# A retention layer and a gated feed-forward on one core: the third value unit by seven quarter products, with new orders of work

## The chip, the core and the metric

The kernel runs on one core of a Trainium2 chip. The metric is device time in microseconds, the median of several executions; the profile is one execution of its own, read from a hardware trace. Five engines work side by side: TensorE (PE in the profile; its weight loads are PEld), VectorE (DVE), ScalarE (ACT), GpSimd (POOL) and SyncE (SP), which here issues transfers. The operands lie in SBUF, TensorE writes into the banks of PSUM, and 16 DMA engines move data to and from HBM.

## The reference, cut to what matters

```python
def _attn_ref(q, k, v):                      # (8, 8, 576, 64) each
    scores = (1 / sqrt(64)) * q @ k.T
    gamma = 1.0 - 2.0 ** (-5.0 - arange(8))  # one per head
    Dmat = where(rel >= 0, gamma ** rel, 0)  # causal decay
    return (scores * Dmat) @ v

def _moe_ref(x, w_gate, w_val, w_out):       # x: (4608, 512), d_ff = 1536
    gate = 1.0 / (1.0 + exp(-(x @ w_gate)))
    val = x @ w_val
    return (gate * val) @ w_out
```

The output of the first, with heads side by side (8 x 576 = 4608 rows of 512 columns), is the `x` of the second.

## The kernel before, in words

**Attention in chunks.** The decay splits into a factor of the query's row and one of the key's, so q and k are scaled by tables (`cast_qk`, L402; from step 11 on the key's factor goes onto v, `cast_v`, L418). A step is 128 rows of one batch; `STEPS` (L101) lists 27 of them, after three pairs of chunks that are handled apart at the start (`PAIRS`). For a step TensorE makes scores (`scores`, L661), a state share k^T v (`products`, L669), masked scores times v (`intra`, L692) and the old state times q (`inter`, L702). VectorE masks (L683) and adds the states in float32 (`add_state`, L821); ScalarE or GpSimd casts them. Steps 0 to 5 go one by one (`slot`), later ones in twos (`slot_of_two`, L733). There, between the first and the second part of `inter`, a *look* (L743) copies one column of each bank of values to a small tile, so that the second part, which writes the same banks, is ordered behind the first.

**Transposes.** Most steps get q and k turned by a transposing transfer on SP (`cross`, L426); steps 0, 1 and 7 by TensorE (`turn_step`, L604).

**Feed-forward in blocks.** Columns of x^T are handled in blocks: 512 first (inside the start-up code, `h_both`, L1323), then two of 256 and seven of 512 (`BLOCKS`, L349). The 512-column blocks from 1024 on use a scheme of seven products in place of eight: the weights of four feature chunks (a *unit*, u = 0, 1, 2) are cut into quarters, and so is the block of x. Sums of weight quarters are made once (`w_sums`, L341), sums of x quarters for each block (`x_sums`, L988). `quarter` (L1046) makes product i of unit u for the gates ("g") or values ("w"): four matmuls of 256 columns, and then on other engines a copy or an addition (ScalarE L1022 and L1067, VectorE L1075 and L1078) and the sigmoid (ScalarE L1061) or the multiply by the gate (VectorE or GpSimd L1063). Gates have three units this way and values two; the third value unit, chunks 8 to 11, is made whole by `value` (L1084): 16 matmuls of 512 columns, and one VectorE multiply for each chunk (L1092). The output product of a block is made in seven products as well (`quarters`, L1121), from sums of gated values (`gv_sum`, L968, on VectorE or GpSimd). Each of these has 12 matmuls of 256 columns.

**What sets the order.** Every instruction is placed by hand. The strings `FIRST`, `ORDER` and `FINAL` (L1101 to L1111) give the order of the quarters in the first, middle and last 512-column block: "g13" is product 3 of gate unit 1, "v9" chunk 9 whole, and what follows a colon are sums of gated values made behind it (unit, part, number, and p for GpSimd or v for VectorE); a v behind the three characters of a quarter puts its multiplies on VectorE. `LATER` puts sums behind the steps of the output products, and `EARLY` begins some quarters of the next block between them. `SUMS_AT` says behind which step of which block a sum of weights is made, and by whom. `SLOT_AT` gives the step from which an attention slot may go; `SOONER` and `keeps` say when output tiles are sent; `CASTS_AT` and `AHEAD` when casts and loads of later steps are issued; `K_ON_POOL` names the steps whose k is cast by GpSimd and not by ScalarE. Engines take their queues in order, so a waiting instruction holds all behind it.

**The start.** TensorE begins with 40 matmuls of 128 columns on a blank tile (`fill`, L233), then 92 of 64 columns (L243), and then turns the first k and q. `fill` stands between later steps of the start too.

```python
fill(10, 4)
SHIFT = 92
for _ in range(SHIFT):
    nc.tensor.matmul(idle[-1][0:64, 0, 0:64], lhsT=blank[0:64, 0:64], rhs=blank[0:64, 0:64], start=True, stop=True)
```

Of the kernel before, what the change touches and what calls it, by code (L numbers as in the profile page):

```python
# [10 lines left out]
BF16 = mybir.dt.bfloat16  # L11
# [5 lines left out]
def kernel(  # L17
# [215 lines left out]
    def fill(n, parts=1):  # L233

        for i in range(n * parts):
            k = 4 // parts
            nc.tensor.matmul(idle[-1][:, 0:k, :], lhsT=blank, rhs=blank.unsqueeze(1).to_broadcast([P, k, P]),
                             start=True, stop=True)

    fill(10, 4)  # L240
    SHIFT = 92
    for _ in range(SHIFT):
        nc.tensor.matmul(idle[-1][0:64, 0, 0:64], lhsT=blank[0:64, 0:64], rhs=blank[0:64, 0:64], start=True, stop=True)  # L243

    def tables(shape, pattern, step, put, fix=None):

# [80 lines left out]
    def value_sums_begin():  # L327

        wt3_sb["w"] = []
        for i in range(3):  # L330
            t = osb.tile([P, NQ, 2, 2 * P], BF16, tag="osb", name=f"wvt_{i}")
            wt3_sb["w"].append([t[:, u] for u in range(NQ)])
            osb.held.append(osb.last)

    def w_quarters(kind, u):

        fa, fb = (slice((4 * u + 2 * y) * P, (4 * u + 2 * y + 2) * P) for y in range(2))
        w = wg_sb if kind == "g" else wv_sb
        return w[:, 0:2, fa], w[:, 2:4, fa], w[:, 0:2, fb], w[:, 2:4, fb]

    def w_sums(kind, i, u, eng):  # L341

        a11, a12, a21, a22 = w_quarters(kind, u)
        s1, s2, s4 = (wt3_sb[kind][j][u] for j in range(3))
        to, a, b, op = ((s1, a21, a22, ALU.add), (s2, s1, a11, ALU.subtract), (a21, a11, a21, ALU.subtract),
                        (s4, a12, s2, ALU.subtract))[i]
        eng.tensor_tensor(out=to, in0=a, in1=b, op=op)

# [64 lines left out]
    SCALED_V = 11  # L413
    X_LATE = "ppvv"
    X_FIRST = "vvvv"
    K_ON_POOL = (11, 13, 15, 16, 19, 21, 23, 26, 27)

    def cast_v(s, eng):  # L418
        natural["v", s] = nat_pool.tile([P, H, D], BF16, tag="v", name=f"v_{s}", bufs=6)
# [313 lines left out]
    def slot_of_two(vals, news):  # L733


        if vals:
            both = vals_tile[vals[0]] = values(len(vals) * M, vals[0])
            for i, s in enumerate(vals):
                val_ps[s] = [t[:, i * M:(i + 1) * M] for t in both]
                intra(s, i == 0)  # L740
                inter(s, [(0,), (1,)])
            for j in range(NJ):
                nc.vector.tensor_copy(out=glance[:, j:j + 1], in_=both[j][:, 0, 0:1])  # L743
        if news:
            rows_tile[news[0]] = row_tiles(ROWS, f"row_{news[0]}")
            for i, s in enumerate(news):
                row_ps[s] = [t[:, i] for t in rows_tile[news[0]]]
                scores(s)
            makes = [s for s in news if STEPS[s][1] < LAST]
            if makes:  # L750
                tiles = row_tiles(ROWS_2, f"new_{makes[0]}")
                for i, s in enumerate(makes):
                    share_ps[s] = [t[:, i] for t in tiles]
                    products(s)
        if not news:
            return
        for s in vals:
            inter(s, [(1,), (0,)])
        mask(*news)
# [108 lines left out]
    pending = []  # L868

    done = {"ld": 0, "cast": 0}  # L870
    AHEAD = (2, 1, 1, 1, 1, 1, 1, 1, 1, 2, 0, 0)

    def loads_to(s):
        while done["ld"] <= min(NS - 1, s):
# [66 lines left out]
    def leave():  # L941
        for at, to in zip(*stores.pop(0)):
            nc.sync.dma_start(out[to, :], at)
# [44 lines left out]
    def x_sums(col, engines):  # L988
# [9 lines left out]
        for (to, a, b), by in zip(((t1, b12, b11), (t3, b22, b12), (t2, b22, t1), (t4, b21, t2)), engines):  # L998
            (nc.gpsimd if by == "p" else nc.vector).tensor_tensor(out=to, in0=a, in1=b, op=ALU.subtract)  # L999

    def quarter_units(gvs, t0):

        BANKS = {("g", 0): [(tr_psum, "tr"), (pv_psum, "pv"), (qk_psum, "qk")],
                 ("g", 1): [(qk_psum, "qk"), (ffn_psum, "ffn"), (st_psum, "st")],
                 ("g", 2): [(pv_psum, "pv"), (st_psum, "st"), (tr_psum, "tr")],
                 ("w", 0): [(ffn_psum, "ffn"), (qk_psum, "qk"), (ffn_psum, "ffn")],
                 ("w", 1): [(ffn_psum, "ffn"), (ffn_psum, "ffn"), (ffn_psum, "ffn")]}
        waiting = []

        def settle():  # L1010
# [20 lines left out]
        def left(kind, u, i):  # L1031
            a11, a12, a21, a22 = w_quarters(kind, u)
            t = wt3_sb[kind]
            return (a11, a12, t[2][u], a22, t[0][u], t[1][u], a21)[i - 1]

        def product(kind, u, i, ps, first):
            w, x = left(kind, u, i), right(i)
# [46 lines left out]
        def value(fc):  # L1084
# [3 lines left out]
            for kc in range(NKC):  # L1088
# [19 lines left out]
    LATER = {}  # L1108
    FINAL = ("g06 g11 w05 g03 w01 g15 g16 g12 g07 w06 g13 g21 g17 w03 g04 w11 w07 w02 g14 w04 g25:0-3p "
             "w16:0-1v g26 w15:0-2v w12:0-4v w17 g22 w13 g27 g23 w14:1-1v v9:1-3v v8 g24 v10 "  # L1110
             "v11:1-2v:1-4v:2-1p:2-2v:2-3v:2-4p").split()  # L1111
    begun = {}

    def gates_early(t0):
# [362 lines left out]
    def op_first(fcs, nbs, opps):  # L1477
        for fc in fcs:
            for nb in nbs:
# [45 lines left out]
    store(opps[3], 3 * P, on_act)  # L1525
    casts_to(1)

    SUMS_AT = ("0.1:w10v 0.2:w11v 0.5:w13v 0.7:g20v 0.8:g21v 0.12:g23v 0.17:o00v 0.17:o10v "
               "1.2:o01v 1.6:o03v 1.9:o11v 1.10:w02v 1.11:o20v 1.13:g12v 1.15:o21v 1.17:o13v "
               "1.17:o23v 2.0:g02v 2.6:o22v 2.9:o02v 2.10:g22v 2.17:w12v 2.43:o12v").split()  # L1530
    sums_at = {}
    for x in SUMS_AT:
        at, x = x.split(":")
# [84 lines left out]
```

## Time and profile before

| | |
|---|---|
| median of 3 runs | 311.12 us (310.93 to 311.51) |
| profiled execution | 311.42 us, its span 309.7 us |
| TensorE busy | 301.5 us, 97% of the span |
| VectorE, ScalarE, GpSimd busy | 231.4, 194.1, 188.0 us |
| five middle blocks (1536 to 3584) | 126.15 to 279.54 us of the span |

The span runs from the first to the last instruction. Rows of groups give line, engine, operation, output and inputs with shapes and count, then busy time and the mean of one in ns, then the idle time of the engine before them and what ended it. Rows by time give start and length in us. Matmuls overlap in the pipeline: one of 256 columns is listed with some 273 ns, while the next starts after about 109.

### The profile page before, as it was taken

How to read it: one execution, taken by the hardware profiler on the slowest of the kernel's cores; microseconds unless marked ns; L12 is line 12 of the kernel's file. 1: busy time of each engine (PE TensorE's matmuls, PEld its weight loads, DVE VectorE, ACT ScalarE, POOL GpSimd, SP SyncE). 2: the span in 40 equal slices, each digit the busy share in tenths (PEclk: the TensorE clock that was granted, in tenths of full speed). 3: DMA queues.
4: the chain of work that ended last, by engine and by line, in shares of the span. 5: the costliest groups of instructions: out<-in, count | busy, mean ns of one | idle time of the engine just before them, and what ended most of it. 6: DMA issues, size and time to landing. Idle time of an engine off the chain costs nothing.

```text
span 309.7 us, 10558 instructions
## 1 busy us (share of the span) xinstructions
PE 301.5 (97%) x4362; PEld 238.2 (77%) x4378; DVE 231.4 (75%) x471; ACT 194.1 (63%) x399; POOL 188.0 (61%) x204
## 2 busy tenths in 40 slices
PE   8899999999999999999999999999999999999995
PEld 8584455876858867886888688868887888788874
DVE  6576877876896986489658965996599659935983
ACT  4666563436439737874797489747964896459730
POOL 5785653653473997945994589458955825550630
PEclk9999999999999999999999999999999999999999
DMA  7999999899999799995299839975994164004003
GB/s 212 315 371 395 356 315 214 194 173 138 226 221 232 123 251 178 206 207 121 40 187 230 230 49 197 264 179 46 225 181 130 38 225 151 2 2 138 1 22 117
DMA packets 145424, 54.99 MB, mean 178 GB/s; under 512 B 124384, under 2 KB 137696, under 8 KB 145376
## 3 DMA queue, kind: packets, MB, share of 16 engines
q1 hardware_dynamic: 144352, 53.66, 73.3%
q8 instruction: 34, 0.56, 0.8%
q10 hardware_dynamic: 1024, 0.66, 0.7%
q14 instruction: 14, 0.11, 0.1%
HBM read 37.75 MB, written 9.44 MB: 152 GB/s over the span
## 4 chain that ended last, share of the span: by engine, by line
PE 84%; DVE 7%; POOL 3%; issue 2%; DMA 1%; SPq 1%; ACT 1%; POOLq 0%; DVEq 0%
PE gatea L1040 11%; PE qa L1154 10%; PE qe L1154 9%; PE wa L1040 7%; PE h L1089 7%; PE gatee L1040 6%; PE we L1040 4%; PE op L1480 3%; PE op L1270 3%; PE gateg L1040 3%; PE hv L1331 3%; PE hg L1331 3%; PE val L697 2%; PE qa L1226 2%; PE wg L1040 2%
## 5 line engine op out<-in xcount | busy, mean ns | idle before, releaser
L973 POOL TENSOR_TENSOR gsum<-gv 128x512 bf16<-128x512 bf16 (+1 forms) x28 | 31.6, 1129 | 21.8 <-DVE gv L1092 14.8
L1063 POOL TENSOR_TENSOR gv<-gv,wu 128x512 bf16<-128x512 bf16 x14 | 16.4, 1172 | 39.0 <-DVE wu L1075 39.0
L1040 PEld LDWEIGHTS <-wg_sb 128*128 128x128 bf16 x336 | 32.9, 98 | 5.6
L1154 PEld LDWEIGHTS <-gsum 128*128 128x128 bf16 x312 | 29.9, 98 | 4.4 <-issue 0.8
L411 POOL TENSOR_TENSOR qk<-q,qtab 128x512 bf16<-128x512 f32 x28 | 30.8, 1099 | 2.0 <-DMA q<-in_q_dram 2.0
L1040 PEld LDWEIGHTS <-wgt_sb 128*128 128x128 bf16 x252 | 24.6, 98 | 3.3
L1075 DVE TENSOR_TENSOR gu<-gatee,gu 128x512 f32<-128x512 f32 x21 | 14.4, 687 | 14.8 <-PE gatee L1040 13.0
L1089 PE MATMUL h<-xT,wv_sb 128*128 128x512 bf16 x105 | 24.9, 379 | 0.4
L1040 PE MATMUL gatea<-xsum,wg_sb 128*128 128x256 bf16 x168 | 25.2, 273 | 0.0
L1154 PEld LDWEIGHTS <-gv 128*128 128x128 bf16 x228 | 21.8, 98 | 4.0
L1040 PEld LDWEIGHTS <-wv_sb 128*128 128x128 bf16 x224 | 21.9, 98 | 2.6
L683 DVE TENSOR_TENSOR pt<-row,tri 128x512 bf16<-128x512 f32 (+1 forms) x36 | 20.0, 596 | 5.1 <-PE row L674 3.9
L411 POOL TENSOR_TENSOR qk<-k,ktab 128x512 bf16<-128x512 f32 x11 | 12.0, 1089 | 19.1 <-DMA k<-in_k_dram 15.6
L1078 DVE TENSOR_TENSOR gs<-gatea,gs 128x512 f32<-128x512 f32 x21 | 14.4, 687 | 9.7 <-PE gatea L1040 8.9
L1061 ACT ACTIVATE gv<-gs 128x512 bf16<-128x512 f32 x21 | 13.4, 640 | 12.5 <-DVE gs L1078 12.5
L422 POOL TENSOR_TENSOR v<-v,ktab 128x512 bf16<-128x512 f32 x19 | 20.5, 1079 | 0.0
L1089 PEld LDWEIGHTS <-wv_sb 128*128 128x128 bf16 x112 | 11.0, 98 | 10.2
L999 POOL TENSOR_TENSOR xsum<-xT 128x512 bf16<-128x512 bf16 x12 | 13.6, 1155 | 8.5 <-ACT xT L770 5.3
L1040 PEld LDWEIGHTS <-wvt 128*128 128x128 bf16 x168 | 16.4, 98 | 2.0
L1092 DVE TENSOR_TENSOR gv<-gv,h 128x512 bf16<-128x512 bf16 x28 | 17.8, 675 | 0.0
L770 ACT CAST xT<-val 128x512 bf16<-128x512 f32 x22 | 12.5, 592 | 8.0 <-PE val L713 8.0
L1040 PE MATMUL wa<-xsum,wv_sb 128*128 128x256 bf16 x112 | 16.8, 272 | 0.0
(195 smaller groups left out, 839.2 us busy)
## 6 DMA issues: line engine op xcount, KB each, us to landing
k<-in_k_dram SPq DMA_DIRECT2D x26, 256.0 KB, 3.9
q<-in_q_dram SPq DMA_DIRECT2D x26, 256.0 KB, 4.2
v<-in_v_dram SPq DMA_DIRECT2D x26, 256.0 KB, 4.5
out_dram<-ob SPq DMA_DIRECT2D x24, 256.0 KB, 3.4
wg<-in_moe_w_gate_dram SPq DMA_DIRECT2D x12, 256.0 KB, 5.3
wv<-in_moe_w_val_dram SPq DMA_DIRECT2D x12, 256.0 KB, 5.1
wo<-in_moe_w_out_dram SPq DMA_DIRECT2D x12, 256.0 KB, 5.0
v32p<-in_v_dram SPq DMA_DIRECT2D x6, 256.0 KB, 5.2
```

The costliest lines, as they stand in the source:

```text
L411: eng.tensor_tensor(out=to, in0=by_halves(loaded[s][1 - i]), in1=tab, op=ALU.mult)
L422: nc.gpsimd.tensor_tensor(out=natural["v", s], in0=loaded[s][2], in1=tab, op=ALU.mult)
L683: nc.vector.tensor_tensor(out=t[:, y, 0:n].rearrange("p i m t -> p (i m) t"), in0=rows_tile[ss[0]][y][:, 0:n].rearrange("p i m t -> p (i m ...
L973: eng.tensor_tensor(out=to, in0=a, in1=b, op=op)
L1040: nc.tensor.matmul(ps[:, f], lhsT=w[:, kc, f * P:(f + 1) * P], rhs=x[:, kc], start=(first and f == 0 and kc == 0), stop=(f == 1 and kc == ...
L1063: eng.tensor_tensor(out=to, in0=to, in1=src, op=ALU.mult)
L1075: nc.vector.tensor_tensor(out=me["u2"], in0=e, in1=me["u2"], op=ALU.add)
L1078: nc.vector.tensor_tensor(out=me["s5"], in0=a, in1=me["s5"], op=ALU.add)
L1089: nc.tensor.matmul(ps, lhsT=wv_sb[:, kc, fc * P:(fc + 1) * P], rhs=xT(kc, slice(t0, t0 + 512)), start=(kc == 0), stop=(kc == NKC - 1))
L1092: nc.vector.tensor_tensor(out=gvs[fc], in0=gvs[fc], in1=ps, op=ALU.mult)
L1154: nc.tensor.matmul(ps[:, b], lhsT=left(fp)[:, b * P:(b + 1) * P], rhs=right(fp), start=(first and fp == 0 and b == 0), stop=(fp == NFC // ...
L1331: nc.tensor.matmul(ps, lhsT=(wg_sb if what == "g" else wv_sb)[:, kc, fc * P:(fc + 1) * P], rhs=xT(kc, slice(0, 4 * P)), start=(kc == 0), s ...
```

## The change

- The third value unit of the five middle blocks (`thirds`) is made by quarters. `ORDER` has w21 to w27 in place of v8 to v11; its sums of weights go into two buffers taken from the ring of output tiles (`last_value_sums_begin`, at the beginning of block 1536) and are made there by VectorE. One of the sums would overwrite a quarter of the weights that the last block still uses whole, so it gets a place of its own (`seventh`). `BANKS` gives the new unit its banks and moves one of the third gate unit's.
- New strings for the middle blocks and the last; sums of gated values partly by halves (a, b) and partly behind the output products (`LATER`). `EARLY` begins two quarters of the next block and not three.
- Looks of seven of the thirteen slots of two go to ScalarE (`LOOK_ACT`).
- The 92 small matmuls are gone. In `h_both`, 48 matmuls of 512 columns are each made as two of 256.
- Other numbers: `K_ON_POOL` (eight steps and not nine), `AHEAD`, `CASTS_AT`, `SLOT_AT`, `SOONER`, and `SUMS_AT`, where five sums go from VectorE to GpSimd. From block 1536 on four output tiles are kept unsent and not six.

```diff
-    fill(10, 4)
-    SHIFT = 92
-    for _ in range(SHIFT):
-        nc.tensor.matmul(idle[-1][0:64, 0, 0:64], lhsT=blank[0:64, 0:64], rhs=blank[0:64, 0:64], start=True, stop=True)
+    FILLS = (10, 0, 0)
+    for n, pieces in zip(FILLS, (4, 2, 1)):
+        fill(n, pieces)
...
+    def seventh(kind, u):
+        return fourth[0] if (kind, u) == ("w", NQ) and fourth else w_quarters(kind, u)[2]
+
+    def last_value_sums_begin():
+        for n in (2, 1):
+            t = osb.tile([P, 2, 2, 2 * P], BF16, tag="osb", name=f"wvt_last_{n}")
+            osb.held.append(osb.last)
+            for i in range(2):
+                (next((x for x in wt3_sb["w"] if len(x) == NQ), fourth)).append(t[:, i])
...
-        to, a, b, op = ((s1, a21, a22, ALU.add), (s2, s1, a11, ALU.subtract), (a21, a11, a21, ALU.subtract),
+        to, a, b, op = ((s1, a21, a22, ALU.add), (s2, s1, a11, ALU.subtract), (seventh(kind, u), a11, a21, ALU.subtract),
...
+    LOOK_ACT = (6, 10, 14, 18, 19, 20, 22, 26, 30, 34)
-    K_ON_POOL = (11, 13, 15, 16, 19, 21, 23, 26, 27)
+    K_ON_POOL = (13, 15, 17, 18, 19, 22, 23, 27)
...
-                nc.vector.tensor_copy(out=glance[:, j:j + 1], in_=both[j][:, 0, 0:1])
+                (on_act if vals[0] in LOOK_ACT else on_dve)(out=glance[:, j:j + 1], in_=both[j][:, 0, 0:1])
...
-    AHEAD = (2, 1, 1, 1, 1, 1, 1, 1, 1, 2, 0, 0)
+    AHEAD = (2, 0, 1, 1, 1, 1, 1, 1, 1, 2, 0, 0)
...
+    def thirds(t0):
+        return BLOCKS[2][0] < t0 < NT - 512
...
-                 ("g", 2): [(pv_psum, "pv"), (st_psum, "st"), (tr_psum, "tr")],
+                 ("g", 2): [(pv_psum, "pv"), (st_psum, "st"), (st_psum, "st") if thirds(t0) else (tr_psum, "tr")],
...
+                 ("w", 2): [(qk_psum, "qk"), (qk_psum, "qk"), (tr_psum, "tr")]}
...
-    EARLY = ((10, "g01"), (12, "g05"), (13, "g02"))
+    EARLY = ((11, "g01"), (13, "g05"))
-    CASTS_AT = (7, 20)
+    CASTS_AT = (2, 23)
...
-    ORDER = ("g06 g11 w05 g03 w01 g15 g16 g12 g07 w06 g13 g21 g17 w03 w11 w07 g04 w02 g14 w04 w16:0-3p "
-             "g26:0-1v w12 w15:0-2v w17v g25 w13 g27 g23:0-4v g22 w14:1-1v v9:1-2v:1-3p g24 v8 v10 "
-             "v11:1-4v:2-1p:2-2p:2-3p:2-4p").split()
-    LATER = {}
+    ORDER = ("g02 g06 g11 w05 g03 w01 g15 g07 g16 g12 w06 g13 w02 g21 g17 w11 w03 w07v g22 g04 g26 w04 "
+             "g25:0a1v:0b1v w16:0a2p:0b2p g14 w12 w15:0a4p:0b3p:0b4p w21 g27:0a3p w17 w13 w22 w26 w25 g23 "
+             "w27 w14 w23 g24 w24:1-1v").split()
+    LATER = {0: ('2-1v',), 1: ('1-2v', '2-2p'), 2: ('2-3p',), 4: ('1-3v',), 9: ('1-4p',), 10: ('2-4p',)}
...
+    CUTS = 48
+    cut = []
...
-                    nc.tensor.matmul(ps, lhsT=(wg_sb if what == "g" else wv_sb)[:, kc, fc * P:(fc + 1) * P],
-                                     rhs=xT(kc, slice(0, 4 * P)), start=(kc == 0), stop=(kc == NKC - 1))
+                    parts = 2 if kc and len(cut) < CUTS else 1
+                    cut.extend([fc] * (parts - 1))
+                    for i in range(parts):
+                        cols = slice(i * 512 // parts, (i + 1) * 512 // parts)
+                        nc.tensor.matmul(ps[:, cols], lhsT=(wg_sb if what == "g" else wv_sb)[:, kc, fc * P:(fc + 1) * P],
+                                         rhs=xT(kc, cols), start=(kc == 0), stop=(kc == NKC - 1 and i == parts - 1),
+                                         skip_group_check=True)
...
-    SUMS_AT = ("0.1:w10v 0.2:w11v 0.5:w13v 0.7:g20v 0.8:g21v 0.12:g23v 0.17:o00v 0.17:o10v "
...
+    SUMS_AT = ("0.0:w10p 0.1:g20v 0.3:w11v 0.6:w13v 0.10:g21v 0.11:o00v 0.14:g23v 0.15:o01p "
...
+               "2.3:o13v 2.3:g02v 2.9:o22v 2.10:g22v 2.13:o02v 2.19:w12v 2.39:o12p 3.0:w20v "
+               "3.2:w21v 3.7:w23v 3.9:w22v").split()
...
-    SLOT_AT = (0, 3, 13, 17, 2, 7)
-    SOONER = (0, -3, 10)
+    SLOT_AT = (2, 0, 12, 13, 2, 7)
+    SOONER = (-4, 3, 8)
...
+        if w == 3:
+            while len(stores) > 4:
+                leave()
+            keeps[0] = 4
+            last_value_sums_begin()
```

More of the change, by code (lines that the diff above doesn't have):

```diff
@@ L333, in value_sums_begin @@
             osb.held.append(osb.last)
+    fourth = []
+    def seventh(kind, u):
[6 more added lines that the diff above has]
+                (next((x for x in wt3_sb["w"] if len(x) == NQ), fourth)).append(t[:, i])
     def w_quarters(kind, u):
@@ L1004, in quarter_units @@
                  ("g", 1): [(qk_psum, "qk"), (ffn_psum, "ffn"), (st_psum, "st")],
-                 ("g", 2): [(pv_psum, "pv"), (st_psum, "st"), (tr_psum, "tr")],
+                 ("g", 2): [(pv_psum, "pv"), (st_psum, "st"), (st_psum, "st") if thirds(t0) else (tr_psum, "tr")],
                  ("w", 0): [(ffn_psum, "ffn"), (qk_psum, "qk"), (ffn_psum, "ffn")],
-                 ("w", 1): [(ffn_psum, "ffn"), (ffn_psum, "ffn"), (ffn_psum, "ffn")]}
+                 ("w", 1): [(ffn_psum, "ffn"), (ffn_psum, "ffn"), (ffn_psum, "ffn")],
+                 ("w", 2): [(qk_psum, "qk"), (qk_psum, "qk"), (tr_psum, "tr")]}
         waiting = []
@@ L1033, in left @@
             t = wt3_sb[kind]
-            return (a11, a12, t[2][u], a22, t[0][u], t[1][u], a21)[i - 1]
+            return (a11, a12, t[2][u], a22, t[0][u], t[1][u], seventh(kind, u))[i - 1]
         def product(kind, u, i, ps, first):
@@ L1104 @@
     LATER_FIRST = {}
-    ORDER = ("g06 g11 w05 g03 w01 g15 g16 g12 g07 w06 g13 g21 g17 w03 w11 w07 g04 w02 g14 w04 w16:0-3p "
-             "g26:0-1v w12 w15:0-2v w17v g25 w13 g27 g23:0-4v g22 w14:1-1v v9:1-2v:1-3p g24 v8 v10 "
-             "v11:1-4v:2-1p:2-2p:2-3p:2-4p").split()
-    LATER = {}
-    FINAL = ("g06 g11 w05 g03 w01 g15 g16 g12 g07 w06 g13 g21 g17 w03 g04 w11 w07 w02 g14 w04 g25:0-3p "
-             "w16:0-1v g26 w15:0-2v w12:0-4v w17 g22 w13 g27 g23 w14:1-1v v9:1-3v v8 g24 v10 "
-             "v11:1-2v:1-4v:2-1p:2-2v:2-3v:2-4p").split()
+    ORDER = ("g02 g06 g11 w05 g03 w01 g15 g07 g16 g12 w06 g13 w02 g21 g17 w11 w03 w07v g22 g04 g26 w04 "
+             "g25:0a1v:0b1v w16:0a2p:0b2p g14 w12 w15:0a4p:0b3p:0b4p w21 g27:0a3p w17 w13 w22 w26 w25 g23 "
+             "w27 w14 w23 g24 w24:1-1v").split()
+    LATER = {0: ('2-1v',), 1: ('1-2v', '2-2p'), 2: ('2-3p',), 4: ('1-3v',), 9: ('1-4p',), 10: ('2-4p',)}
+    FINAL = ("g06 g11 w05 g03 g02 w01 g15 g16 g12 g07 w06 g13 g21 g17 w11 w03 w07 g14 g04 w02 w04 "
+             "w16:0-1v:0-3v g26 w12 w15 w17:0-2p:0-4v g25 g22 w13 g23 g27 w14:1-1p v9:1-3p v8 g24:1-2v v10 "
+             "v11:1-4v:2-1v:2-2p:2-3v:2-4p").split()
     begun = {}
@@ L1526 @@
     casts_to(1)
-    SUMS_AT = ("0.1:w10v 0.2:w11v 0.5:w13v 0.7:g20v 0.8:g21v 0.12:g23v 0.17:o00v 0.17:o10v "
-               "1.2:o01v 1.6:o03v 1.9:o11v 1.10:w02v 1.11:o20v 1.13:g12v 1.15:o21v 1.17:o13v "
-               "1.17:o23v 2.0:g02v 2.6:o22v 2.9:o02v 2.10:g22v 2.17:w12v 2.43:o12v").split()
+    SUMS_AT = ("0.0:w10p 0.1:g20v 0.3:w11v 0.6:w13v 0.10:g21v 0.11:o00v 0.14:g23v 0.15:o01p "
+               "0.16:o10p 1.3:o11v 1.5:o03p 1.6:o20v 1.8:w02v 1.12:g12v 1.14:o21v 1.17:o23v "
+               "2.3:o13v 2.3:g02v 2.9:o22v 2.10:g22v 2.13:o02v 2.19:w12v 2.39:o12p 3.0:w20v "
+               "3.2:w21v 3.7:w23v 3.9:w22v").split()
     sums_at = {}
```

## The prediction

> **What bounds the kernel now.** I read the page first: busy times, then the chain that ended last.
>
> ```profile
> span 309.7 us, 10558 instructions
> PE 301.5 (97%) x4362; PEld 238.2 (77%) x4378; DVE 231.4 (75%) x471; ACT 194.1 (63%) x399; POOL 188.0 (61%) x204
> PE 84%; DVE 7%; POOL 3%; issue 2%; DMA 1%; SPq 1%; ACT 1%; POOLq 0%; DVEq 0%
> q8 instruction: 34, 0.56, 0.8%
> ```
>
> TensorE is busy for 97% and is 84% of the chain. A busy PE need not be a full one, so I asked for stretches (TensorE, weight load, VectorE, ScalarE, GpSimd, then clock, DMA share, GB/s):
>
> ```profile
> 17.00:54.00 37.00, 36.63 (x351) 20.39 (x354) 27.97 (x51) 19.75 (x40) 21.34 (x32) 1.00 1.05 333
> 54.00:92.75 38.75, 37.75 (x679) 28.30 (x682) 31.54 (x75) 18.18 (x50) 21.00 (x23) 1.00 1.05 189
> 92.75:126.15 33.40, 32.32 (x486) 27.04 (x485) 26.22 (x53) 23.20 (x46) 25.30 (x27) 1.00 0.93 195
> 126.15:279.54 153.39, 153.07 (x2349) 128.06 (x2353) 114.97 (x225) 108.01 (x217) 101.36 (x95) 1.00 0.65 144
> 279.54:309.70 30.16, 26.67 (x228) 22.02 (x226) 19.55 (x36) 15.35 (x31) 8.23 (x7) 0.99 0.23 71
> ```
>
> The fourth row is the five middle blocks: 30.68 us each, TensorE idle for 0.32 us in all five. There time goes only by taking columns off TensorE, and comes back by any wait that a new order makes. From 54 to 126 it idles 2.08 us. The DMA engines are full until 92.75 and have room afterwards.
>
> **The change, part by part.** The chain's rows give the rates (start, length, count):
>
> ```profile
> 141.06 2.59 PE h L1089 x12
> 143.65 1.31 PE qa L1154 x12
> 179.72 1.31 PE qe L1154 x12
> 121.14 0.59 issue
> ```
>
> *Third value unit.* Now 16 products of 512 columns at 2.59/12 = 0.2158 us: 3.45 us a block. After: 7 quarter products of 4 matmuls at 1.31/12 = 0.1092: 28 x 0.1092 = 3.06. Gain 0.39 a block, 1.97 in five, all on the path. *48 split products:* 48 x (2 x 0.1092 - 0.2158) = +0.12; their extra weight loads (98 ns each) hide under 109 ns matmuls.
>
> What the unit costs the others (count, then busy, mean ns):
>
> ```profile
> L1040 PE MATMUL wa<-xsum,wvt 128*128 128x256 bf16 x56 | 8.4, 273 | 0.0
> L1040 PEld LDWEIGHTS <-wvt 128*128 128x128 bf16 x168 | 16.4, 98 | 2.0
> L1067 ACT COPY wg<-wa 128x512 f32<-128x512 f32 x14 | 8.4, 597 | 0.0
> L1078 DVE TENSOR_TENSOR ws<-wa,ws 128x512 f32<-128x512 f32 x14 | 9.6, 689 | 0.7 <-PE wa L1040 0.5
> L1092 DVE TENSOR_TENSOR gv<-gv,h 128x512 bf16<-128x512 bf16 x28 | 17.8, 675 | 0.0
> L1063 POOL TENSOR_TENSOR gv<-gv,wu 128x512 bf16<-128x512 bf16 x14 | 16.4, 1172 | 39.0 <-DVE wu L1075 39.0
> L973 POOL TENSOR_TENSOR gsum<-gv 128x512 bf16<-128x512 bf16 x24 | 29.0, 1206 | 21.5 <-DVE gv L1092 14.4 <-DVE gv L1063 7.0
> L973 POOL TENSOR_TENSOR gsum<-gv 128x256 bf16<-128x256 bf16 x4 | 2.7, 665 | 0.3 <-DVE gv L1092 0.3
> L743 DVE COPY glance<-val 128x1 f32<-128x1 f32 x26 | 2.9, 153 | 14.0 <-PE val L713 13.8
> ```
>
> By the order of instructions, per block: ScalarE +3 copies = 1.8 us; VectorE +2 adds, +2 multiplies, -4 multiplies of `value`, about 0; GpSimd +2 multiplies (2.3), and 4 whole plus 6 half sums in place of 6 whole (8.8 against 7.2): +3.9. Means per block were 21.6 (ScalarE), 23.0 (VectorE), 20.3 (GpSimd): 23.4, 23 and 24.2 of some 30.3, so no engine runs out; what counts is latency at the block's end.
>
> *The block's end.* Quarters now run up to `w24`, and its multiply on VectorE writes rows that the first output product reads. Rows for the rates:
>
> ```profile
> 174.22 1.47 PE L1154 MATMUL qa<-wo_sb,gv 128*128 128x256 bf16 x12
> 173.89 1.87 DVE L1092 TENSOR_TENSOR gv<-gv,h 128x512 bf16<-128x512 bf16 x3
> L973 DVE TENSOR_TENSOR gsum<-gv,gsum 128x512 bf16<-128x512 bf16 x14 | 7.7, 549 | 0.0
> L683 DVE TENSOR_TENSOR pt<-row,tri 128x512 bf16<-128x512 f32 x24 | 15.4, 685 | 1.2 <-PE new L674 0.2
> L831 DVE TENSOR_TENSOR s<-s,new 128x256 f32<-128x256 f32 x30 | 12.5, 416 | 1.2
> ```
>
> VectorE starts one such operation every (1.87 - 0.675)/2 = 0.60 us. Take the start of the output products as 0. Product `g23` is sixth from the end, so its last matmul ends at -5 x 0.437 + 0.164 = -2.02. From it VectorE has five operations without a pause (g23, w27, w14, w23, w24): the fifth starts at about -1.98 + 4 x 0.60 = 0.42 and ends at 1.11. TensorE wants it for matmul 11, at 10 x 0.109 = 1.09, its weights (98 ns) sooner: a wait of about 0.15, 0.75 in five blocks. Ends: 0, and 0.45 a block if operations follow each other at their full 0.689. I take 0.15, by the packed row above. Second, the sum `2-1v` now stands on VectorE behind GpSimd's last multiply of unit 2, and behind that sum queue all that the next attention slot needs: GpSimd's four multiplies of 1.17, after its half sums, end at about +2.1; two sums (0.549 each), two masks (0.685, the second 0.60 on) and four state adds (0.416, some 0.45 apart) bring VectorE to 6.3, and ScalarE's cast of the state (0.6, as its copies) to 6.6 or 6.9 less the part that runs beside the last adds. TensorE needs them some 0.2 after the second attention slot begins, at 179.72 + 1.31 - 174.22 = 6.8. Cost 0, with some 0.35 of cover; what it costs beyond that is the third rival.
>
> *Looks on ScalarE* take 153 ns operations off VectorE in half the slots; TensorE waits for a look only after the slot's score and state products, so cost 0; without that cover it is one ScalarE operation ahead of the look, 0.6 a slot. *K casts:* one more on ScalarE, which has room, 0. *Four sums of the third unit* come once, in the first of the five blocks, on VectorE, which has 7 us a block to spare (114.97 of 153.39): 0, or their 4 x 0.549 = 2.2 if they stood ahead of adds that TensorE waits for. Other sums go from VectorE to GpSimd (w10, o01, o03, o10, o12), two or three to a block where GpSimd is busy for 21.00 of 38.75: 0. The two held buffers shorten the ring of output tiles; their stores are issued when only four are left waiting instead of six, on SP's queue ahead of later loads, with the DMA engines at 0.65: 0. The second number of `AHEAD` asks for a load that the first has already issued: 0. `g02` is no longer begun early but opens the next order, at the same place in TensorE's stream; FINAL takes its units in a somewhat other order, FIRST is unchanged: 0.
>
> *Slots of block 512.* Slots 0 and 1 come two units later, 2 and 3 one unit sooner (a unit is 8 matmuls of 256 columns, 0.87 us). Each issues the casts and loads of the step three on, and its transpose on SP. GpSimd and SP take these in queue order and wait there for landings, not for TensorE, so their times hardly move; the sooner slots eat 0.87 of their cover, as below.
>
> *No small idle matmuls.* The front, by time (start, length):
>
> ```profile
> 1.05 4.45 PE L237 MATMUL idle<-blank 128*128 128x128 bf16 x40 [1.05 <-DVE blank L224]
> 3.77 1.04 POOL L394 TENSOR_TENSOR kp<-k32p,ktab 128x512 bf16<-128x512 f32 x1 [0.83 <-ACT ktab L257]
> 4.42 0.94 DVE L394 TENSOR_TENSOR qp<-q32p,qtab 128x512 bf16<-128x512 f32 x1
> 5.43 3.10 PE L243 MATMUL idle<-blank 64*64 64x64 bf16 x92
> 8.46 0.40 PE L446 MATMUL kTp<-ident,kp 128*128 128x128 bf16 x4
> 10.69 1.29 DVE L472 TENSOR_TENSOR ptp<-qkp,trip 128x512 bf16<-128x512 f32 x2 [2.88 <-PE qkp L465]
> 11.70 3.20 POOL L391 CAST vp<-v32p 128x512 bf16<-128x512 f32 x4 [1.41 <-DMA v32p<-in_v_dram]
> 14.85 0.61 POOL L305 CAST wg_sb<-wg 128x512 bf16<-128x512 f32 x1
> 15.16 0.62 PE L502 MATMUL st<-vp,kp 64*128 64x128 bf16 x8
> 18.24 0.61 PE L1395 MATMUL hg<-xT,wg_sb 128*128 128x256 bf16 x4
> ```
>
> K and q are cast by 4.81 and 5.36; their transposes start only at 8.46, behind the 92. Without these the transposes, and VectorE's chain from 10.69 on, start 3.0 us sooner. What is late next is V: two of four casts end at 11.70 + 2 x 0.80 = 13.30, fed by DMA, and the state product of 15.16 cannot go earlier: 1.8. The gate weights, cast by 15.46, allow 2.8 for 18.24. So 1.8 stays, between 0 and 3.0; I take 1.8 as the last operand's row sets it. Further on DMA is the cover to watch:
>
> ```profile
> DMA to landing us min/median/max: 2.8/4.2/6.0
> 73.45 1.30 SPq L428 DMA_TRANSPOSE T<-qk  x1
> 81.66 0.30 PE L666 MATMUL row<-T 64*64 64x64 bf16 x16
> ```
>
> Of block 768's transposes this one stands nearest before its use. Even at the slowest landing, 6.0, it is there at 79.45, 2.2 before its scores; 1.8 fits, with 0.4 left. Slots 2 and 3, sooner by 1.8 + 0.87, use transposes issued a whole slot earlier, with more cover than that.
>
> *The gap of 0.59 us* at 121 follows a dense stretch of small products and names no engine. Instruction packets are 0.56 MB/34 = 16 KB; counted in the order, the gap lies where one such packet had been used up by small products alone. Moved counts spread that stretch over two packets: -0.59. Ends: 0, or the same gap in other slots. The Trainium skill, "Runtime: NRT & Kernel Launch", section "Instruction fetch mechanics", says refills come in 16 KiB blocks and are mostly hidden; the packets agree, the gap does not, and by that rule alone this term would be 0 and the sum 0.6 higher.
>
> **Sum.** 311.42 (profiled execution; 1.72 of it lies outside the span) - 1.97 + 0.12 + 0.75 - 1.80 - 0.59 = 307.93. The median shown, 311.12, is 0.30 below that execution: 307.6.
>
> **The rivals.**
> - *The front is given back:* loads set a later step, nothing remains of 1.8: 309.4. For it: a DMA share of 1.05 up to 92.75. Against: the covers above.
> - *The clock falls back:* with fewer dense matmuls early, TensorE drops to the rate of its first 40 (4.45/40 = 0.111 us for 128 columns, twice 0.1092/2). One more such spell in dense work costs half of 4.45: 309.8. Against: fills stay between the transposes, and every stretch shows 1.00. The Trainium skill, "TensorE: Matmul & The Clock Gate", section "Part 4: PE-mode transpose", says transposes don't count as activity, which is what would do it; no run here shows it.
> - *Slower:* GpSimd's chain at the block's end runs late. Up to 0.35 is covered; a whole further multiply (1.17) costs 0.82 a block, 4.1 in five: 311.7. Beyond 1.05 us of lateness the change gains nothing; at 1.4 it is 312.9. For it: +3.9 us on GpSimd, and 39.0 us that it already waits on VectorE's adds.
> - *More closes up:* no wait at the blocks' ends, and most of the other 1.5 us of idle between 54 and 126 goes: 305.5.
>
> **How the numbers follow.** Forecast 0.52, front given back 0.15, clock 0.05, closes up 0.10, GpSimd late 0.18, of which a few hundredths end level. The range 305.3 to 311.3 takes in all but most of the last; the likeliest case's own is 306.3 to 308.8 (waits of 0 to 0.45 a block, gap kept or not). A change within 0.2%, 0.6 us, is about what can't be told from none: faster 0.80, level 0.05, slower 0.15.
>
> **What would show it.** Right: the five blocks take about 152.2 us, first state product near 13.4, no issue gap near 119, waits below 0.2 at each first output product. Wrong: waits in the second slots behind VectorE, first dense products still at 18, or issue gaps in several slots.

## The result, and the profile after

The changed kernel takes 307.6 us (median; 306.25 to 308.15) against 311.02 for the one before on the same chip: a ratio of 0.9883, 95% interval 0.9861 to 0.9905. Its profiled execution took 307.6, with a span of 305.7. Medians are of all executions; the ratios leave out the few that ran in a second, slower state of the chip. First the page of the changed kernel: span, busy times, the chain that ended last, and the queue of instruction packets.

```profile
span 305.7 us, 10621 instructions
PE 298.8 (98%) x4394; PEld 245.9 (80%) x4394; DVE 232.2 (76%) x454; ACT 204.4 (67%) x429; POOL 214.7 (70%) x240
PE 80%; DMA 11%; SPq 3%; DVE 2%; POOL 1%; issue 1%; ACT 0%; DVEq 0%
q8 instruction: 34, 0.56, 0.8%
```

TensorE is 2.7 us less busy, GpSimd 26.7 us more. 11% of the chain now lies in transfers, where it was 1%: in this execution the front of the kernel has become a matter of loads. The same stretches as before, in the changed kernel (stretch, its length; then busy time and count of TensorE, weight load, VectorE, ScalarE, GpSimd; clock, DMA share, GB/s):

```profile
52.17:89.85 37.68, 37.68 (x683) 28.16 (x681) 30.00 (x72) 18.26 (x51) 25.56 (x27) 1.00 1.04 201
89.85:122.73 32.88, 32.64 (x486) 26.91 (x485) 29.33 (x53) 23.64 (x49) 26.94 (x28) 1.00 1.02 208
122.73:274.98 152.25, 151.62 (x2410) 133.59 (x2409) 117.94 (x215) 116.89 (x243) 121.82 (x126) 1.00 0.63 147
274.98:305.70 30.72, 27.23 (x233) 22.42 (x230) 18.53 (x36) 15.96 (x32) 10.51 (x9) 1.00 0.23 70
```

The first block of quarters begins at 89.85 instead of 92.75 (-2.90). The next stretch is 0.52 shorter, the five middle blocks 1.14, the last 0.56 longer, and 0.18 more lies outside the span: together -3.82, the difference of the two profiled executions. One correction: the last block's `g02` used to stand ahead of the mark that parts the third row from the fourth, and stands behind it in the new `FINAL`; its four matmuls of 0.109 (0.44 us) went from one row to the other. The middle blocks' own gain is therefore 0.70 and the last stretch's loss 0.12.

TensorE's waits in the changed kernel (total, times, longest):

```profile
PE qkp L479 <- ACT qT L470: 0.6, 2, 0.4
PE new L688 <- issue: 0.4, 1, 0.4
PE turn L624 <- DVE apart L580: 0.4, 1, 0.4
PE st L516 <- POOL vp L404: 0.3, 1, 0.3
PE val L727 <- issue: 0.2, 1, 0.2
```

Of what was to show the forecast wrong one thing is there: the issue gap at 121 is gone, but two others have appeared inside attention slots of the second and fourth middle block. By time, the first of them (start, length; in brackets the idle time before):

```profile
172.35 0.41 PE L688 MATMUL new<-v,qk 64*64 64x64 bf16 x25
173.15 0.25 PE L688 MATMUL new<-v,qk 64*64 64x64 bf16 x7 [0.39 <-issue]
```

A group of 32 products stops after 25, with all its operands there. At the block's end, the first output product of each middle block on the chain (start, length, count; the first and the last of five):

```profile
139.81 1.38 PE qa L1173 x12
...
262.65 1.38 PE qa L1173 x12
```

1.38 against 1.31 without a wait: 0.07 a block. The first of them by time, with the VectorE multiply that it waits for:

```profile
139.65 1.55 PE L1173 MATMUL qa<-wo_sb,gv 128*128 128x256 bf16 x12
140.07 0.68 DVE L1082 TENSOR_TENSOR gv<-gv,wa 128x512 bf16<-128x512 bf16 x1
```

The front, by time:

```profile
1.05 4.45 PE L237 MATMUL idle<-blank 128*128 128x128 bf16 x40 [1.05 <-DVE blank L224]
5.29 0.47 PE L460 MATMUL kTp<-ident,kp 128*128 128x128 bf16 x4
10.88 1.38 POOL L404 CAST vp<-v32p 128x512 bf16<-128x512 f32 x2 [0.23 <-DMA v32p<-in_v_dram]
12.05 0.64 PE L516 MATMUL st<-vp,kp 64*128 64x128 bf16 x8
14.09 0.61 POOL L404 CAST vp<-v32p 128x512 bf16<-128x512 f32 x1 [1.05 <-DMA v32p<-in_v_dram]
14.75 0.38 PE L516 MATMUL st<-vp,kp 64*128 64x128 bf16 x7 [0.30 <-POOL vp L404]
15.66 0.61 PE L1422 MATMUL hg<-xT,wg_sb 128*128 128x256 bf16 x4
...
89.68 0.60 PE L1059 MATMUL gatea<-xT,wg_sb 128*128 128x256 bf16 x4
```

Transposes start 3.17 sooner, the first state product 3.11 (at 12.05, where the forecast has 13.4), the first dense products 2.58; the last cast of V, and the state product behind it, wait for a transfer.

### The profile page after: what moved, and what is told of

Same layout as the page of the kernel before. It is cut to its first block, busy times and chain, and to the rows that moved or that the text cites. A ratio compares the mean times of both kernels' runs of the same rounds, so it can differ in the third digit from the quotient of the medians.

```text
span 305.7 us, 10621 instructions
## 1 busy us (share of the span) xinstructions
PE 298.8 (98%) x4394; PEld 245.9 (80%) x4394; DVE 232.2 (76%) x454; ACT 204.4 (67%) x429; POOL 214.7 (70%) x240
## 4 chain that ended last, share of the span: by engine, by line
PE 80%; DMA 11%; SPq 3%; DVE 2%; POOL 1%; issue 1%; ACT 0%; DVEq 0%
PE gatea L1059 11%; PE qa L1173 11%; PE wa L1059 10%; PE qe L1173 9%; PE gatee L1059 6%; PE we L1059 5%; DMA wg<-in_moe_w_gate_dram 4%; PE h_g L930 3%; PE h_v L930 3%; PE op L1289 3%; PE gateg L1059 3%; PE wg L1059 2%; SPq L182 2%; PE h L1108 2%; DMA v<-in_v_dram 2%; PE val L711 2%
## 5 line engine op out<-in xcount | busy, mean ns | idle before, releaser
L1082 POOL TENSOR_TENSOR gv<-gv,wu 128x512 bf16<-128x512 bf16 x19 | 22.1, 1163 | 26.6 <-DVE wu L1094 26.6
L1059 PEld LDWEIGHTS <-wv_sb 128*128 128x128 bf16 x284 | 27.8, 98 | 3.3
L987 POOL TENSOR_TENSOR gsum<-gsum,gv 128x256 bf16<-128x256 bf16 (+1 forms) x19 | 16.6, 886 | 13.8 <-DVE gsum L987 11.5
L436 POOL TENSOR_TENSOR v<-v,ktab 128x512 bf16<-128x512 f32 x19 | 21.4, 1125 | 0.0
L987 POOL TENSOR_TENSOR gsum<-gv,gsum 128x256 bf16<-128x256 bf16 (+1 forms) x23 | 20.9, 915 | 0.1
L987 POOL TENSOR_TENSOR gsum<-gv 128x256 bf16<-128x256 bf16 (+1 forms) x23 | 20.0, 871 | 0.8 <-DVE gv L1111 0.3
L1059 PE MATMUL wa<-xsum,wv_sb 128*128 128x256 bf16 x132 | 19.8, 273 | 0.0
L1080 ACT ACTIVATE gv<-gu 128x512 bf16<-128x512 f32 x21 | 13.4, 637 | 6.2 <-DVE gu L1094 6.2
L1082 POOL TENSOR_TENSOR gv<-gv,ws 128x512 bf16<-128x512 bf16 x14 | 16.6, 1185 | 0.4 <-DVE ws L1097 0.4
```

The lines of the kernel that those rows point to most:

```text
L436: nc.gpsimd.tensor_tensor(out=natural["v", s], in0=loaded[s][2], in1=tab, op=ALU.mult)
L1059: nc.tensor.matmul(ps[:, f], lhsT=w[:, kc, f * P:(f + 1) * P], rhs=x[:, kc], start=(first and f == 0 and kc == 0), stop=(f == 1 and kc == ...
L1080: nc.scalar.activation(out=to, in_=src, func=AF.Sigmoid)
L1082: eng.tensor_tensor(out=to, in0=to, in1=src, op=ALU.mult)
```

## The experiments

All were compared with the kernel before on the chip on which they ran, where that took 310.7 to 311.0. Intervals are 95%; two kernels of the study can be told apart only from some 0.3 to 0.5% on.

**The front alone.** The kernel before with `SHIFT = 0`:

```diff
-    SHIFT = 92
+    SHIFT = 0
```

> The kernel before without its 92 small idle matmuls, nothing else. Front: 1.9 (A) or 2.9 us (B) sooner by about 90 us. The 184 instructions fewer also move every later packet boundary. If issue gaps belong to packets used up by dense small products, the gap of 0.59 at 121 us goes, and five packets of 256 instructions now hold so many of them that they last only 2.6 to 3.6 us: gaps of 0.2 to 1.2 us in the first slots of the first two middle blocks and in second slots, 0.4 to 2.3 in all. Time then 308.0 to 310.8. Rival, the gap at 121 belongs to that place and not to packets: it stays, alone, and the time is 309.1 (A) or 308.1 (B).

Measured: 308.65 us, 0.9912 (0.9875 to 0.9949). Its stretches, at the same marks:

```profile
89.96:122.55 32.59, 32.16 (x487) 26.97 (x485) 27.85 (x55) 23.18 (x46) 24.57 (x26) 1.00 0.91 209
122.55:276.03 153.48, 153.36 (x2355) 128.12 (x2353) 115.03 (x226) 107.94 (x217) 102.22 (x96) 1.00 0.69 144
```

The first block of quarters begins at 89.96: the front gave 2.79 here without any of the other edits, so nearly all of the 2.90 is the front's (view B) and not the new orders'. Both are single executions, and the start of that block varies by more than the difference (see the account of the front below). The gap at 121 is gone too (33.40 to 32.59), which speaks for packets; but of the five gaps that I thought possible only one is there, 0.12 us at 148.06. This edit is 2.2 of the 3.4 us by medians, 2.7 of 3.6 by the ratios.

**The front taken back.** The changed kernel with small idle products ahead of the first transposes, 128 of them (256 instructions), so that all later packets stay as they are. First with 40 columns, then again with 64:

```diff
+    for _ in range(128):
+        nc.tensor.matmul(idle[-1][0:64, 0, 0:40], lhsT=blank[0:64, 0:64], rhs=blank[0:64, 0:40], start=True, stop=True)
```

> The changed kernel with small idle matmuls put back ahead of the first transposes: 128 of 40 columns, about as long as the 92 of 64 columns were (3.1 us) and 256 instructions, so that every later instruction keeps its place in its 16 KB packet. Theory A, the front is limited by what comes after the transposes: the loss is what the front gave, 1.9 us by the last rows before 54 us (309.5), and the 1.0 us that the stretch from 54 to 92 us gave stays, because it belongs to the new orders. Theory B, the front gave all 2.9 us up to 92: 310.5. Rival, the front is given back at a later load: 307.6. In all three the two issue gaps (0.5 and 0.4 us) stay in the dense slots of the second and fourth middle block.

> The changed kernel with 128 small idle products of 64 columns ahead of the first transposes (4.3 us by the 92's 3.1, every later instruction keeping its place in its packet). The first run of this kind had 40 columns and took 7.0 us for its 128, which came out at the end of TensorE's work as 6.8. If TensorE's front is the limit all the way, the loss is the start of the transposes moved, some 4.3: 311.9. If loads took the limit over at the forecast's point, 1.8 of the 3.1 lost and no more: 309.4 to 310.6.

Measured: with 40 columns 313.14 us (309.78 to 315.94), 1.0023 (0.9981 to 1.0064); with 64 columns 310.35, 0.9984 (0.9964 to 1.0004). The second, by time, has its transposes 3.70 later than the changed kernel:

```profile
1.05 3.84 PE L237 MATMUL idle<-blank 128*128 128x128 bf16 x40 [1.05 <-DVE blank L224]
4.82 4.24 PE L244 MATMUL idle<-blank 64*64 64x64 bf16 x128
8.99 0.40 PE L462 MATMUL kTp<-ident,kp 128*128 128x128 bf16 x4
```

Of the 3.7 us 2.7 are lost by the medians and 3.1 by the ratios: TensorE's start is passed on, less 0.6 to 1 us. That is between my two views, nearer to the larger. That the rest is taken up by loads is likely, not shown: this run's chain is 96% TensorE and has no share of DMA, where the changed kernel's first profile has 11%, but a second one of the changed kernel (below) has none either. The run with 40 columns was no measurement of that: its 128 products took 7.01 us, and more came out slow:

```profile
5.43 7.01 PE L244 MATMUL idle<-blank 64*64 64x40 bf16 x128
12.38 0.61 PE L462 MATMUL kTp<-ident,kp 128*128 128x128 bf16 x4
13.21 1.49 PE L237 MATMUL idle<-blank 128*128 128x512 bf16 x3
17.91 0.42 PE L481 MATMUL qkp<-qT,kT 64*64 64x128 bf16 x16
```

Four transposes take 0.61 there and 0.40 in the other run; three idle products of 512 columns 1.49, in the changed kernel 0.81. TensorE ran at half rate until about 17 us (at 17.91 it is at full rate), though the page's row of the granted clock shows full speed (9, 90% or more) in every slice:

```profile
PEclk9999999999999999999999999999999999999999
```

With 40 columns of a quarter of the array TensorE was busy without a pause, and yet the rate did not rise.

**The clock.** The 40 first idle products of 128 columns made small (64 of 64):

> The changed kernel with its 40 first idle products (128 columns, 4.45 us) as 40 small ones (64 of 64 columns, some 1.4 us), so that the places of all instructions stay and TensorE sits idle from about 2.5 to 4.9 us. The forecast's rival, the clock falls back: without the dense start the granted clock in the next slices is below 1.00, and one spell of 4.45 us at half rate costs 2.2: 309.8. Other view, the clock doesn't depend on them, or not long, and the first transposes start 0.4 sooner, at 4.85 behind the K casts: 307.2 to 307.6, the front being fed by loads from there on.

```diff
-    for n, pieces in zip(FILLS, (4, 2, 1)):
-        fill(n, pieces)
+    for _ in range(40):
+        nc.tensor.matmul(idle[-1][0:64, 0, 0:64], lhsT=blank[0:64, 0:64], rhs=blank[0:64, 0:64], start=True, stop=True)
```

Measured: 307.46, 0.9901 (0.9862 to 0.9939): not to be told from the changed kernel.

```profile
4.87 0.61 PE L460 MATMUL kTp<-ident,kp 128*128 128x128 bf16 x4 [1.49 <-POOL kp L407]
5.82 1.49 PE L237 MATMUL idle<-blank 128*128 128x512 bf16 x3
7.81 0.40 PE L460 MATMUL kTp<-ident,kp 128*128 128x128 bf16 x4
```

The half rate is over at 7.81 here, at 5.63 in the changed kernel, and costs nothing that can be measured. The first state product is 0.36 later (12.41), but the second, which in the changed kernel has to wait for the last cast of V until 14.75, is through at 14.96 here and at 15.13 there. The rival's mechanism exists; no price of it can be measured here. The Trainium skill, "TensorE: Matmul & The Clock Gate", section "Part 1: The HAM clock gate", says the full rate comes after about 3.4 us of activity, counted in a window that runs by itself. The traces lie around that: of the 40 products, begun at 1.05, those from 4.1 us on ran at full rate in the execution in which they took 3.84 us, and none did where they took 4.45. In the one profile with 7 us of small products and no rise, not every activity counted.

**The packets.** The changed kernel with half the splits, so that everything later lies 48 instructions earlier in its packet:

```diff
-    CUTS = 48
+    CUTS = 24
```

> The changed kernel with 24 split products instead of 48: 0.06 us less work, and every later instruction 48 places sooner in its packet. If issue gaps come from packets that dense small products use up faster than the next packet arrives: by the order of instructions four packets now last 2.5, 1.3, 2.1 and 2.5 us (in the dense slots near 141, 172, 208 and 238 us). The gaps of 0.5 and 0.4 us in the changed kernel came in packets that last 3.7 and 3.3 us, packets of 2.9 us passed without one, so a packet takes some 2.9 to 4.2 us: gaps of 0.4 to 1.7, 1.6 to 2.9, 0.8 to 2.1 and 0.4 to 1.7 us there, together 3.2 to 8.4 in place of 0.95: 309.8 to 315, I take 311.5. Rival, the gaps are something else that the profile doesn't name: they stay where they are, 307.5.

Measured: 308.95, 0.9911 (0.9879 to 0.9944). On the chain, the rows around the gaps:

```profile
173.64 1.57 issue
175.21 1.36 PE qe L1173 x11
...
211.04 0.54 issue
211.58 1.36 PE qa L1173 x11
```

Both old gaps are gone, and two of the four named slots have new ones, the largest where the shortest packet was (1.3 us). The time is below the range that I gave (309.8 to 315) and the sum of the gaps less than I took, because I had the time of a packet wrong. With the packets' transfers of the trace it comes out (times in us, worked out from the trace; a packet is entered where the order has its first instruction, "next starts" is the time from there to the start of the next packet's transfer, "until use" runs from that transfer's end; "stands" is the time between two starts beyond the usual spacing, a little more than the trace's idle time):

```
kernel          packet  lasts  next starts  takes  TensorE stands  until use
before          3263    3.1    1.8          0.9    0.8             1.2
changed         4799    3.7    1.9          0.9    0.5             1.4
changed         7103    3.4    1.2          1.0    0.4             1.6
changed         5823    3.1    0.3          1.0    0               -
24 splits       4799    1.3    0.8          0.9    1.75            1.4
24 splits       6079    2.2    0.7          1.0    0.7             1.3
24 splits       3775    2.6    0.2          0.9    0               -
changed, again  5823    3.1    1.8          0.9    0.9             1.3
changed, again  4799    3.7    1.6          0.9    0.1             1.3
```

In these rows the next packet is of use about 1.4 us after its transfer, which takes 0.9 to 1.0; what varies is the 0.2 to 1.9 us until the transfer starts. A packet that lasts less than the sum of the three makes a gap. (Elsewhere in the traces a transfer took up to 2.5 us, and some began up to 1.1 us before the packet ahead was entered.) The places of the gaps say the same. Nine traces of kernels without the 92 have a record of every product; in them ten idle times of 0.1 us or more with nothing to wait for lie behind 54 us, and ahead of each TensorE has 193 records more than a multiple of 256: 4289, 5057, 5313, 6081, 6337 or 7361. The changed kernel again:

> The changed kernel again, to stand beside the others on the same chip: 307.6 by its first runs. If issue gaps come from waiting until the packet's transfer starts (0.2 to 1.9 us after it is asked for in the traces so far, then 0.9 to 1.3 us for itself and 1.4 us until TensorE goes on), the packets that last 3.7 and 3.3 us (near 172 and 238 us) show gaps that differ from execution to execution, 0 to 0.8 us, and no other place shows one above 0.3. Rival, the gaps are a property of those slots: again 0.5 and 0.4.

Measured: 307.66 (306.39 to 308.3), 0.9883 (0.9849 to 0.9917). The gap moved once more; here are the issue row of the chain, from the page the shares of the chain, and by time the first matmul of the first block of quarters:

```profile
202.80 0.76 issue
```

```profile
PE 97%; ACT 1%; issue 0%; DVE 0%
```

```profile
88.76 0.60 PE L1059 MATMUL gatea<-xT,wg_sb 128*128 128x256 bf16 x4
```

That is the packet of 3.1 us in the third middle block, which had passed without one; the other two show 0.1 and 0. My text allowed gaps in two packets only and was wrong in that; that the gaps differ between executions, held. The chain has no share of DMA in this execution, and that matmul starts at 88.76, where it started at 89.68 in the first profile: the front was done 0.9 sooner, most of what this execution, 306.39, is below the other's 307.6. Then the gaps were removed: 59 splits, and the four first score products written several times over in five slots, so that by the order no packet from 54 us on lasts under 4.0:

```diff
+    REPEATS = {12: 4, 16: 2, 18: 2, 20: 2, 22: 1}
...
-        for m in range(M):
+        for m in [0] * REPEATS.get(s, 0) + list(range(M)):
...
-    CUTS = 48
+    CUTS = 59
```

> The changed kernel with 59 instead of 48 split products and 44 score products written twice in five slots (0.46 us of work in all), which moves every dense slot across a packet boundary so that no packet of TensorE's instructions from 54 us on lasts under 4.0 us by the order of instructions. If the gaps are packets used up before the next one is there, no issue gap above 0.15 us is left after 54 us; the four profiles of kernels with the changed kernel's packets had 0.4 to 1.1 us of them, so the time is 0.1 to 0.6 below the changed kernel's 307.6: 307.0 to 307.5, and its executions lie closer together. Rival, gaps come from elsewhere: they stay, and the work is added: 308.1.

Measured: 307.18 (306.19 to 308.93), 0.9888 (0.9862 to 0.9913). The chain has no issue row left in the middle blocks, and TensorE no idle time there:

```profile
121.85:273.53 151.68, 151.68 (x2454) 133.78 (x2453) 117.63 (x215) 116.87 (x243) 121.80 (x126) 1.00 0.65 148
```

(Three rows of 0.16 us ahead of 90 us stand where the trace lacks the record of one product.) So the gaps are packets. The time is where it was expected but can't be told from the changed kernel's, and the executions lie no closer together: the spread of some 2 us is not made by the gaps. The front, 0.9 us apart in two executions of one kernel, is a likely part of it. Another is outside the span: 1.9 us in the changed kernel, 1.9 to 3.1 in the executions of this one. Its spans have a median of 304.35 against 305.7, so more was won inside than the times show; in its profile one more packet is transferred at 306.1, after the span's end at 304.25, but that this is the cause is not shown, and the run with both harmless edits below repeats neither (305.5 inside, 1.7 to 1.9 outside). The rest stays open.

**The looks.** The changed kernel with all looks on VectorE (`LOOK_ACT = ()`), and the kernel before without its 92, with the changed kernel's looks on ScalarE:

> The changed kernel with all looks back on VectorE. Forecast's view, the looks hide behind the slot's score and state products: 307.6, within 0.3. Rival, VectorE's 0.15 us per look stands ahead of the masks that TensorE waits for: up to 0.15 us in each of the ten slots, 309.1, to be seen as waits of the slot's products behind VectorE.

> The kernel before without its 92 small idle matmuls, with the changed kernel's looks on ScalarE. With all looks on VectorE the changed kernel took 309.8 with 2.4 us of waits behind them, the kernel before without the 92 took 308.65 with 0.6. View A, the looks only hurt because the third unit by quarters fills VectorE's queue at the blocks' ends: here they are worth at most those 0.6: 308.0 to 308.7. Rival, moving the looks is a gain by itself and the third unit adds little: 307.6 or below, as the changed kernel.

Measured: 309.78, 0.9954 (0.9923 to 0.9985), and 309.23, 0.9942 (0.9921 to 0.9962). The second lies above both ranges of my text. In the first, TensorE waits for the looks (who waited for them: us, times; then the longest of these waits by time), and the middle blocks are 2.14 longer than the changed kernel's:

```profile
PE val L727: 2.4, 6
267.24 0.32 PE L727 MATMUL val<-T,sb 64*64 64x64 bf16 x16 [0.59 <-DVE glance L757]
122.97:277.36 154.39, 152.26 (x2411) 133.82 (x2409) 120.16 (x227) 115.80 (x231) 121.94 (x126) 1.00 0.62 144
```

With the third unit in quarters, VectorE's queue at a block's end is long enough for looks in it to be late, by 0.4 us once in each of the five middle blocks, 2.14 in all. (The sixth wait, 0.28 at 112 us, is there with the unit whole as well: 0.43 at 114 in the kernel before.) This profile has no issue gaps, so against a kernel without gaps the looks cost more, by the rows some 3 us. Without the unit the middle blocks have no such waits, and the move brings little: the wait of 0.43 us at 111.65 goes, but ahead of it this profile already runs 0.97 later than that of the front alone, and the ratio is 0.9942 beside 0.9912. So the looks belong to the third unit: with both the ratio is 0.9883, with neither 0.9912, with the unit and its new orders alone 0.9954. The intervals of the last two overlap, so that the unit alone loses is likely and not certain; the waits are in the rows.

**GpSimd at the block's end.** `2-1v` made `2-1p` in `LATER`:

> The changed kernel with one sum of unit 2 at the end of each block (2-1) on GpSimd instead of VectorE: GpSimd's chain there is 1.21 us longer, VectorE's one operation of 0.55 shorter. The forecast's rival, GpSimd late: beyond a cover of 0.35 each us of lateness costs a us a block, so 0.86 in five blocks, +4.3, 311.9, with waits of the second slots behind VectorE and GpSimd. Other view, VectorE's queue alone sets that time and the sums of unit 2 aren't wanted until the output products of the middle: no loss, 307.3 to 307.7.

Measured: 307.31, 0.9882 (0.9845 to 0.9918). A whole sum more on GpSimd's chain costs nothing that can be measured, and its trace has no wait of the second slots behind VectorE or GpSimd. The edit also takes 0.55 off VectorE, so it bounds the two together; 0.35 of cover on GpSimd's chain alone would have shown. Both harmless edits with the repeats:

> The same as the run before with the two harmless edits of the earlier runs added: the sum 2-1 on GpSimd and the first 40 idle products short. Each alone took 307.3 and 307.5 against 307.6, no difference that can be told; together with the gaps gone 306.5 to 307.4. If one of them was a loss hidden in the spread, 307.6 or above.

Measured: 307.25, 0.9895 (0.9868 to 0.9921). Within the range, and no faster than the repeats alone: none of these versions can be told from the changed kernel.

## Why the prediction came out right

The path was right: columns off TensorE, a shorter front, a moved gap, a small wait at the blocks' ends. That the time fell on the forecast's very number is luck: the front and the blocks' ends gave more than forecast, and new issue gaps took about as much back.

- *Third unit:* the columns are as counted; the 0.12 of the splits, which lie in the front, can't be seen in any run. With the middle blocks of before at 153.39, less 1.97 and 0.44 (`g02`), plus 0.35 for the blocks' ends and 0.88 for the two gaps (0.48 and 0.40), one gets 152.21; the row says 152.25. The forecast had 152.2 for it from other terms, so that sign shows little. With the gaps taken out and 0.46 of repeated products, 151.79 against 151.68.
- *Block's end:* 0.07 a block where the step said 0.15, 0.35 and not 0.75. The mechanism, the last multiply just late for its matmul, is as described, and VectorE was where the step put it: in the rows above the multiply runs from 0.42 to 1.10 after the output products begin. Its weight load came 0.17 late, and the matmul lost 0.07 of that, since the other loads here begin 0.11 ahead of their matmuls; the step counted the load's whole lateness.
- *Front:* the step that failed is "the state product of 15.16 cannot go earlier" than two casts of V. It needs the first only, and that cast, which ended at 12.31 before, ended by 11.67; the product went at 12.05, while the second cast ran on to 12.26. Instead of 1.8 the front gave 2.9, and 2.8 with nothing else changed. In the ten profiles of kernels with neither the 92 nor the 128 the first block of quarters begins 1.8 to 3.8 us sooner than in the one profile of before, 2.8 in the middle, so 1.8 was the low end. That something else then takes over is right, but later than I put it: of 3.7 us of later start 2.7 to 3.1 come out at the end.
- *Issue gap:* -0.59 where it was, but +0.88 in other slots. I had named this end of the range ("the same gap in other slots") and did not count the other dense slots against the packet boundaries, which the order of instructions allowed. Six profiles with the changed kernel's packets have 0.25 to 1.1 us of idle time in such gaps, so the term should have been about 0, between -0.3 and +0.5, and not -0.59.
- *Sum of the differences:* the front, with the splits in it, gave 1.2 more than forecast, the blocks' ends 0.4 more, the gaps 0.9 less; another 0.3 was lost in the last stretch and outside the span.
- *Rivals:* the front was not given back. GpSimd late is refuted by the run with a longer chain; what I called its cover seems to have been VectorE's, and VectorE's own queue was the thing near its limit, as the looks show. I priced the looks at 0, which holds for the kernel as it is; undone, the step costs 2.2 us by medians, and it should have been written as the condition of the third unit's gain. The clock did not fall, but my argument against it, that every stretch shows 1.00 (the last shows 0.99), was no argument: the page's row shows full speed in the run where TensorE was at half rate for 16 us.

## What to carry to other kernels

Price a saved column only after asking which short operation now stands behind the new ones in the queue of the engine that finishes the block: here a move of 153 ns looks was worth some 2 us, as much as the columns. Where a trace has issue gaps with all operands there, count instructions against packets of 256 before changing anything earlier in the program, because every inserted or removed instruction moves them. Idle products at the start can be serving the clock, the packets, or neither; take them out and read the spacing of the first real products, not the granted clock.

## What the runs showed of the hardware

- TensorE can use up 256 instructions, 128 of them small products, in 1.3 us, and then stands for up to 1.75 us: in the packets listed the next one's transfer starts 0.2 to 1.9 us after the packet before is entered, takes 0.9 to 1.0, and its instructions run some 1.4 later. The Trainium skill, "Runtime: NRT & Kernel Launch", section "Instruction fetch mechanics", calls refills mostly hidden. For packets of full-array products alone that holds here, where no gap was seen; for packets dense with 64x64 products it does not.
- 128 products of 64 rows and 40 columns, without a pause, took 54 ns each and left TensorE at half rate; 128 of 64 columns, begun after it had risen, took 32 ns each. At half rate 64 columns take 53 ns as well (the run with 40 short ones), so the width does not set that time, and whether 64 columns would have raised the rate is not shown. That the first kind left the rate low was seen in one profile; the spread of that kernel's times, 309.8 to 314.4 without the slowest two, suggests that it sometimes rises.
